# Splitting the first four loads of a gated attention-and-MLP kernel into two half transfers each, with a shorter TensorE filler

## The chip, the cores and the metric

The kernel runs on one core of one Trainium2 chip. The metric is device time in microseconds (us) of one execution of the whole program. Three runs of the kernel before took 259.8, 259.92 and 260.26 us, a median of 259.92 us.

## The reference, cut to what matters

The input x has 2048 tokens of 640 features in bf16. A gate g is the sigmoid of the row sum of x times gate_w. The output is g times a plus (1 - g) times b.

- a is linear attention with 32 heads of 20 features. qkv is x @ wqkv (640 by 1920), phi(t) is t + 1 for t > 0 and exp(t) otherwise, plus 1e-6. pk-transposed times v gives a 20 by 20 matrix per head, pq times that is divided by pq times the column sum of pk, and the result goes through wo.
- b is a two-part mixer: layernorm, w1, gelu, a shift of the four feature quarters by 1, -1, 2, -2 tokens, w2, residual; then layernorm, w3 (640 to 1728), gelu, w4, residual.

The part that this case touches is the beginning of a: q = x @ wq, where wq is the first 640 columns of wqkv.

```
qkv = (x @ wqkv).reshape(B, S, 3, H, Dh)
pq, pk = phi(q), phi(k)
```

## The kernel before, in words

**Tiling.** Tokens are cut into 16 tiles of 128 rows, features into 5 slices of 128. TensorE contracts over 128 partitions, so q for one token tile is the sum of five steps, one for each feature slice k: the transposed x tile `xT[:, k, tile]` as weights, the weight slice `wq[:, k, :]` as the moving operand, 512 columns and then 128 columns into two PSUM banks. So a step needs the x tile, transposed, and rows 128k to 128k+127 of wq.

**Loads.** Lines 694 to 715 issue the loads in a fixed order, each with a semaphore of its own, on the queue of SyncE (SP) or that of ScalarE (ACT). SP has, in order, x0, x1, wq2, x2, wk0, x3, wk2, wk4, x4, then a DMA transpose of x tile 3 (`x_turn`, line 690), which waits for x3, then the rest of x. ACT has wq0, wq1, wq3, wq4, wk1, wk3, and its first activation comes after them. Each of these loads is 128 rows of 1280 bytes, 160 KB. GpSimd (POOL) loads gate_w and fills small constants. ScalarE and SyncE issue their transfers by instructions of their own, in program order.

**TensorE's order in the first stage.** It is written out by hand (lines 945 to 950). `warmup` (line 871) issues filler matmuls on constants, which need no load: `WARM` = 3456 columns (line 770) as six matmuls of 512 columns and three of 128. Then `t_x(0)` (line 773) transposes x tile 0 by TensorE, first one block of 128 columns into one bank and then four into another, and VectorE copies each out to `xT` (line 779). After a second filler of 128 columns (`WARM2`) comes `q_three` (line 930), whose order is

```
order = [(0, 0), (1, None), (0, 1), (1, 0), (1, 1), (0, 2), (1, 2), (0, 3), (2, None), (1, 3), (0, 4), (1, 4),
         (2, 0), (2, 1), (2, 2), (2, 3), (2, 4)]
```

where (t, k) is the step of token tile t with slice k, and (t, None) is the transposing of tile t. `stream` (line 907) issues these; lines 923 and 924 are the 512-column and the 128-column matmul of a step. Then `k_two` does the same for k with the wk slices (`wkg` in the profile) and `k_tile(2)` follows; from tile 3 on, q and k alternate and the DMA transposes supply `xT`.

**The planner.** The order of everything else is chosen while the program is built: `_Items.run` (line 336) takes, again and again, the item that a cost model says can start first on TensorE. That model (`simulate`, line 232) charges an issue of 500 ns and 330 bytes per ns to each load, and 0.834 ns a column to the first filler; so the loads and the filler are inputs to it. The PSUM bank of an item is chosen by the same model. Semaphore waits follow from a tracker of which rows and bytes each instruction reads and writes (`_collect`, line 122); at the end of the program GpSimd waits once on each load's semaphore (line 309).

Of the kernel before, what the change touches and what calls it, by code (L numbers as in the profile page):

```python
# [11 lines left out]
D = 640  # L12
# [404 lines left out]
def _build(nc, A_x, A_wqkv, A_wo, B_w1, B_w2, B_w3, B_w4, gate_w, out, dbg=None, stop=None):  # L417
    sch = _Sched(nc)
# [59 lines left out]
    x_tok = pa.alloc("x_tok", [128, NT, D], BF16)  # L478
# [20 lines left out]
    wq = ra.alloc("wq", [128, KD, D], BF16)  # L499
# [77 lines left out]
    def dve(fn, reads, writes, cost=None):  # L577
        if cost is None:
            n = nfree(writes[0])
            cost = 65.0 + n / 0.96  # L580
        return sch.op("dve", fn, reads, writes, cost=cost)
# [93 lines left out]
    x2 = A_x[0]  # L675

    def dma_in(out_ap, in_ap, key, **kw):
        return sch.dma("sp", out_ap, in_ap, key, **kw)

    def load_x(t):  # L680
        dma_in(x_tok[:, t, :], x2[128 * t:128 * (t + 1), :], "x%d" % t)

    def load_wq(k, queue):
        sch.dma(queue, wq[:, k, :], A_wqkv[128 * k:128 * (k + 1), 0:D], "wq%d" % k)
# [6 lines left out]

    gwr = xn[:, 1, 0:128]
    dve(lambda e: e.memset(gwr, 0.0), [], [gwr])
    load_x(0)
    load_wq(0, "act")
    load_x(1)
    load_wq(1, "act")
    load_wq(2, "sp")
    load_wq(3, "act")
    load_x(2)  # L700
# [66 lines left out]
        assert tags.get((buf, sl)) == what, ("stale ring slot", buf, sl, what, tags.get((buf, sl)))  # L767

    IT = _Items()
    WARM = 3456  # L770
    WARM2 = 128

    def t_x(t):
        for k0, k1 in ((0, 1), (1, KD)) if t < 2 else ((0, KD),):
            b = bank()
            tr_group(b, [x_tok[:, t, 128 * k:128 * (k + 1)] for k in range(k0, k1)])
            if t == 2:
                mm_group(ps[:, b, 448:448 + KD], [(gwr, ident[:, 0:KD])])
            copy(dve, xT[:, k0:k1, 128 * t:128 * (t + 1)], psb(b, 0, 128 * (k1 - k0)).rearrange("p (k c) -> p k c", k=k1 - k0))
            if t == 2:  # L780
                copy(dve, wkg[:, :, D + 1:D + 2], ps[:, b, 448:448 + KD].rearrange("p (k o) -> p k o", o=1))
# [89 lines left out]
    def warmup(cols, cyc):  # L871
        b = bank()
        one = nc.const_aps.tensor(1.0, [128, 512], BF16)
        steps = [512] * (cols // 512) + [128] * (cols % 512 // 128)

        def fn(e):
            ins = None
            for n in steps:
                ins = e.matmul(ps[:, b, 0:n], one[:, 0:128], one[:, 0:n], start=True, stop=True)
            return ins  # L880
        pe(fn, [], [ps[:, b, :]], cost=cols * cyc)
# [60 lines left out]
    def addA(name, dur, fn, deps=()):  # L942
        IT.add("A", name, dur, fn, deps)

    addA(("warm",), 0.0, lambda: warmup(WARM, 0.834))
    addA(("tx", 0), 0.28, lambda: t_x(0))
# [478 lines left out]
def bass_gated_mix__linear_attn_block__mixer_s_mlp__prompt_kernel(  # L1425
    nc, A_x, A_wqkv, A_wo, B_x, B_w1, B_w2, B_w3, B_w4, gate_w, out
):
    assert tuple(A_x.shape) == (1, S, D) and tuple(out.shape) == (1, S, D)
    assert tuple(A_wqkv.shape) == (D, 3 * D) and tuple(A_wo.shape) == (D, D)
    assert tuple(B_w1.shape) == (D, D) and tuple(B_w2.shape) == (D, D)  # L1430
    assert tuple(B_w3.shape) == (D, F) and tuple(B_w4.shape) == (F, D) and tuple(gate_w.shape) == (D,)
    _build(nc, A_x, A_wqkv, A_wo, B_w1, B_w2, B_w3, B_w4, gate_w, out)
# [28 lines left out]
```

## Time and profile before

| what | value |
|---|---|
| three runs | 259.8, 259.92, 260.26 us |
| median | 259.92 us |
| profiled execution, first to last instruction (the only time recorded of it) | 258.2 us |
| median less that span | 1.7 us |
| TensorE busy | 253.3 us, 98% of the span |
| VectorE, ScalarE, GpSimd busy | 144.1, 108.2, 90.2 us |
| bytes read from HBM, written | 12.04 MB, 2.62 MB |

In the profile's rows a time is counted from the first instruction of the span, "PE" is a TensorE matmul, "PEld" its weight load, "SPq" and "ACTq" are the queues on which SyncE and ScalarE issue transfers. A matmul's duration is modelled with its pipeline's tail, so the rate of TensorE is read from the spacing of its rows and not from their durations. The bracket at the end of a row tells how long the engine sat idle before it and what ended that.

### The profile page before, as it was taken

To read this page: it belongs to the slowest core of one execution; us is meant where nothing else is said; L and a number is where in the kernel's file an instruction comes from. 1 tells how busy PE (TensorE), PEld (TensorE's weight loads), DVE (VectorE), ACT (ScalarE), POOL (GpSimd) and SP (SyncE) were. 2 spreads that over 40 slices of the span, in tenths; PEclk is the share of its full clock that TensorE was granted. 3 is DMA by queue.
4 is the path that set the end of the run, shared out by engine and by line. 5 is a ranking of instruction groups with operands and counts; after the bars stand their busy time and mean duration, and the time that the engine had idled before them with its cause. 6 is when DMAs were issued, how large, how long until landed. Compare 5 with 4: busy or idle time off the path is not lost.

```text
span 258.2 us, 3930 instructions
## 1 busy us (share of the span) xinstructions
PE 253.3 (98%) x1485; PEld 126.3 (49%) x1512; DVE 144.1 (56%) x284; ACT 108.2 (42%) x221; POOL 90.2 (35%) x144
## 2 busy tenths in 40 slices
PE   8999999999999999999999999999999999999996
PEld 3555555544454554555444445444444744445554
DVE  2588888899963993679999600399600033200023
ACT  1396676751366868675854331001540100253000
POOL 5012399967952152658917000133100021300000
PEclk9999999999999999999999999999999999999999
DMA  7766699646636699454636630114200022200011
GB/s 220 209 152 208 119 162 201 185 93 127 126 77 79 120 393 301 85 85 71 127 49 108 122 63 3 30 25 127 53 0 0 3 55 77 102 3 0 0 53 52
DMA packets 55891, 26.25 MB, mean 102 GB/s; under 512 B 47252, under 2 KB 54461, under 8 KB 55872
## 3 DMA queue, kind: packets, MB, share of 16 engines
q1 hardware_dynamic: 53696, 21.61, 37.4%
q0 software_dynamic: 1168, 3.28, 5.9%
q10 hardware_dynamic: 1008, 1.11, 1.2%
q8 instruction: 12, 0.20, 0.3%
q14 instruction: 7, 0.06, 0.1%
HBM read 12.04 MB, written 2.62 MB: 57 GB/s over the span
## 4 chain that ended last, share of the span: by engine, by line
PE 95%; DMA 2%; ACT 1%; issue 1%; DVE 0%; SPq 0%
PE ps L604 51%; PE ps L1216 30%; PE ps L806 8%; DMA wq<-in_A_wqkv_dram 2%; PE ps L923 2%; PE ps L1251 1%; ACT hsT L660 1%; PE ps L1129 1%; PE ps L924 1%; DVE x_tok L643 0%; PE ps L1010 0%; PE ps L1039 0%; ACT junk L659 0%; SPq L285 0%; PE ps L615 0%
## 5 line engine op out<-in xcount | busy, mean ns | idle before, releaser
L604 PE MATMUL ps<-xnT,w 128*128 128x512 bf16 x350 | 80.0, 379 | 0.5 <-issue 0.2
L643 DVE SCALAR_TENSOR_TENSOR x_tok<-ps,stg,abx 128x512 bf16<-128x512 f32 (+1 forms) x20 | 13.3, 670 | 80.6 <-PE ps L1216 58.6
L660 ACT ACTIVATE h2T<-ps 128x512 bf16<-128x512 f32 x52 | 30.5, 598 | 61.6 <-PE ps L604 61.5
L604 PEld LDWEIGHTS ps<-xnT,w 128*128 128x128 bf16 x360 | 34.6, 98 | 39.7 <-issue 0.5
L1216 PE MATMUL ps<-w,h2T 128*128 128x512 bf16 (+1 forms) x254 | 47.7, 346 | 0.3
L626 POOL TENSOR_SCALAR xn<-x_tok,st 128x640 bf16<-128x640 bf16 x32 | 35.1, 1105 | 26.0 <-DMA xnT<-xn 25.3
L626 POOL TENSOR_SCALAR abx<-x_tok,stg 128x640 f32<-128x640 bf16 x16 | 15.0, 945 | 70.8 <-DVE x_tok L643 70.8
L1216 PEld LDWEIGHTS ps<-w,h2T 128*128 128x128 bf16 x260 | 23.2, 98 | 24.5 <-issue 0.3
L660 ACT ACTIVATE Er<-ps 128x640 bf16<-128x640 f32 (+1 forms) x35 | 22.9, 662 | 15.4 <-PE ps L604 10.0
L659 ACT ACTIVATE junk<-x_tok 128x640 bf16<-128x640 bf16 x32 | 23.6, 739 | 2.8 <-DVE x_tok L641 2.5
L660 ACT ACTIVATE hsT<-ps 128x512 bf16<-128x512 f32 (+1 forms) x32 | 19.0, 594 | 11.2 <-PE ps L604 10.8
L604 PE MATMUL ps<-w,hsT 128*128 128x128 bf16 (+1 forms) x159 | 23.5, 298 | 0.2
L604 PE MATMUL ps<-wkg,xT 128*128 128x512 bf16 (+1 forms) x138 | 21.3, 298 | 0.1
L641 DVE SCALAR_TENSOR_TENSOR x_tok<-ps,x_tok 128x640 bf16<-128x640 f32 x16 | 13.1, 821 | 12.2 <-ACT junk L659 7.7
L1216 PE MATMUL ps<-M_sb,pqnT 128*128 128x512 bf16 (+1 forms) x98 | 19.6, 347 | 0.1
L604 PEld LDWEIGHTS ps<-w,hsT 128*128 128x128 bf16 x160 | 13.3, 98 | 12.3
L1158 DVE TENSOR_TENSOR pq_tok<-pq_tok,dnr 128x300 bf16<-128x300 bf16 (+1 forms) x48 | 17.7, 421 | 0.6
L806 PE MATMUL ps<-pk_tok,x_tok 128*128 128x512 bf16 x78 | 17.6, 379 | 0.1
L604 PEld LDWEIGHTS ps<-wkg,xT 128*128 128x128 bf16 x140 | 11.9, 97 | 11.2
L634 DVE TENSOR_TENSOR qprod<-qprod,pk_tok 128x640 f32<-128x640 f32 x13 | 16.3, 1252 | 0.5
L604 PE MATMUL ps<-wq,xT 128*128 128x512 bf16 (+1 forms) x69 | 16.2, 367 | 0.1
L626 DVE TENSOR_SCALAR Er<-Er 128x640 bf16<-128x640 bf16 (+1 forms) x35 | 12.1, 346 | 6.9 <-ACT Er L660 6.3
(89 smaller groups left out, 235.7 us busy)
## 6 DMA issues: line engine op xcount, KB each, us to landing
w<-in_B_w_dram SPq DMA_DIRECT2D x1, 2160.0 KB, 9.8
w<-in_B_w_dram SPq DMA_DIRECT2D x1, 2080.0 KB, 15.4
out_dram<-x_tok SPq DMA_DIRECT2D x3, 640.0 KB, 3.2
x_tok<-in_A_x_dram SPq DMA_DIRECT2D x1, 1280.0 KB, 6.5
w<-in_B_w_dram POOLq DMA_DIRECT2D x8, 160.0 KB, 4.5
x_tok<-in_A_x_dram SPq DMA_DIRECT2D x5, 160.0 KB, 5.2
wv<-in_A_wqkv_dram POOLq DMA_DIRECT2D x1, 800.0 KB, 5.6
wq<-in_A_wqkv_dram ACTq DMA_DIRECT2D x4, 160.0 KB, 4.3
```

The source lines that it names most:

```text
L604: ins = e.matmul(out_ap, l, r, start=(i == 0), stop=(i == n - 1))
L626: return engf(lambda e: e.tensor_scalar(out_ap, in_ap, s1, s2, op0, op1), rd, [out_ap], cost=cost)
L634: return engf(lambda e: e.tensor_tensor(out_ap, a, b_, op), [a, b_], [out_ap], cost=cost)
L641: return dve(lambda e: e.scalar_tensor_tensor(out_ap, in0, scalar, in1, op0, op1, accum_out=accum), rd, [out_ap, accum], cost=cost + 70.0)
L643: return dve(lambda e: e.scalar_tensor_tensor(out_ap, in0, scalar, in1, op0, op1), rd, [out_ap], cost=cost)
L659: return act(lambda e: e.activation(out_ap, in_ap, func, bias=bias, scale=scale, accum_out=accum), rd, wr, cost=cost)
L660: return act(lambda e: e.activation(out_ap, in_ap, func, bias=bias, scale=scale), rd, wr, cost=cost)
L806: ins = e.matmul(o, l, r, start=(t0 + q_ == 0), stop=(t0 + q_ == NT - 1))
L923: e.matmul(ps[:, b, 0:512], l, w[:, k, 0:512], start=(k == 0), stop=(k == KD - 1))
L924: return e.matmul(ps[:, b + 1, 0:n2], l, w[:, k, 512:512 + n2], start=(k == 0), stop=(k == KD - 1))
L1158: dve(lambda e, o=o, i0=i0, i1=i1: e.tensor_tensor(o, i0, i1, ALU.mult), [i0, dnr[:, 1, sd, :]], [o], cost=cost)
L1216: ins = e.matmul(o, l, r, start=first and i == 0, stop=last and i == len(prs) - 1, skip_group_check=True)
```

## The change

The four loads x0, wq0, x1, wq1 become eight. Each is cut into rows 0 to 63 and rows 64 to 127; the first half goes on SyncE's queue and the second on ScalarE's, each with its own semaphore. The order on both queues is x0, wq0, x1, wq1; all later loads keep their queue and order behind them. The first filler is 2944 columns, that is five matmuls of 512 and three of 128. Nothing else in the source differs.

```diff
-    load_x(0)
-    load_wq(0, "act")
-    load_x(1)
-    load_wq(1, "act")
+    for t in range(2):
+        for dst, src, key in ((x_tok[:, t, :], x2[128 * t:128 * (t + 1), :], "x%d" % t),
+                              (wq[:, t, :], A_wqkv[128 * t:128 * (t + 1), 0:D], "wq%d" % t)):
+            for h, queue in enumerate(("sp", "act")):
+                rows = slice(64 * h, 64 * (h + 1))
+                sch.dma(queue, dst[rows], src[rows], "%s%s" % (key, "ab"[h]))
     load_wq(2, "sp")
     load_wq(3, "act")
     load_x(2)
@@
-    WARM = 3456
+    WARM = 2944
```

## The prediction

> **What bounds the kernel now.** I read the page's shares first, then the chain of work that ended last, then the first 9 us engine by engine, and last the DMA issues with their time to landing. From the page:
>
> ```profile
> PE 253.3 (98%) x1485; PEld 126.3 (49%) x1512; DVE 144.1 (56%) x284; ACT 108.2 (42%) x221; POOL 90.2 (35%) x144
> PE 95%; DMA 2%; ACT 1%; issue 1%; DVE 0%; SPq 0%
> ```
>
> TensorE is the bound, so the change can pay only where TensorE waits. The chain, asked for the first 8 us, says where that is:
>
> ```profile
> 0.79 0.40 SPq L285
> 1.26 0.41 SPq L285
> 1.71 4.82 DMA wq<-in_A_wqkv_dram
> 6.57 0.39 PE ps L923
> ...
> 7.56 0.36 PE ps L615 x5
> ```
>
> The reader is to see that the end hangs neither on x0, x1, wq0 or wq1 nor on the filler. It hangs on the load that SP issues third, wq2, out at 1.71 and in at about 6.52; from 6.57 on the chain is TensorE. TensorE's own rows, and ScalarE's:
>
> ```profile
> 0.83 3.04 PE L879 MATMUL ps<-const-bfloat16-1.0 128*128 128x512 bf16 x9 [0.83 <-PEq L1446]
> ...
> 5.71 0.39 PE L923 MATMUL ps<-wq,xT 128*128 128x512 bf16 x1
> 5.93 0.22 PE L924 MATMUL ps<-wq,xT 128*128 128x128 bf16 x1
> 6.57 0.39 PE L923 MATMUL ps<-wq,xT 128*128 128x512 bf16 x1 [0.42 <-DMA wq<-in_A_wqkv_dram]
> ...
> 7.47 0.45 PE L615 MATMUL ps<-ident,x_tok 128*128 128x128 bf16 x5
> ```
> ```profile
> 1.21 0.15 PEld L879 LDWEIGHTS ps<-const-bfloat16-1.0 128*128 128x128 bf16 x1 [0.27 <-issue]
> 1.64 0.15 PEld L879 LDWEIGHTS ps<-const-bfloat16-1.0 128*128 128x128 bf16 x1 [0.28 <-issue]
> ...
> 3.81 0.28 PEld L615 LDWEIGHTS ps<-ident,x_tok 128*128 128x128 bf16 x5 [0.22 <-DMA x_tok<-in_A_x_dram]
> ```
> ```profile
> 3.65 1.28 ACT L660 ACT_TABLE_LOAD   x1 [3.65 <-issue]
> 8.53 1.30 ACT L660 ACTIVATE Er<-ps 128x640 bf16<-128x640 f32 x2 [3.59 <-PE ps L924]
> ```
>
> To be seen: the filler's rows stand 0.43 us apart for 512 columns; the last filler row starts at 3.56; tile 0 is transposed from 3.81, when x0 is in; step (1,1) starts at 5.71; step (0,2) waits for wq2 until 6.57; tile 2 is transposed at 7.47, just after x2 lands. Last the loads and the load on the DMA engines:
>
> ```profile
> x_tok<-in_A_x_dram SPq DMA_DIRECT2D x1, 160.0 KB, 3.0
> wq<-in_A_wqkv_dram ACTq DMA_DIRECT2D x1, 160.0 KB, 3.2
> wq<-in_A_wqkv_dram SPq DMA_DIRECT2D x1, 160.0 KB, 4.8
> ...
> x_tok<-in_A_x_dram SPq DMA_DIRECT2D x1, 160.0 KB, 5.2
> ```
> ```profile
> 3.00:4.00 1.00, 1.00 (x9) 0.50 (x7) 0.00 (x0) 0.35 (x1) 0.84 (x4) 1.00 1.06 386
> 7.00:8.00 1.00, 1.00 (x12) 0.57 (x10) 0.01 (x1) 0.00 (x0) 0.00 (x0) 1.00 1.06 383
> ```
>
> The last two columns of the second fence are the busy share of the 16 DMA engines and GB/s. From 3 to 8 us the engines are full at 310 to 386 GB/s: loads are served out of a backlog, and what lands when is decided by the bytes ahead of it.
>
> **The change part by part.** By the trace's landing records x0 is whole at 3.77, wq0 3.95, x1 4.51, wq1 4.78, wq2 6.52, wq3 6.73, x2 7.42, wq4 7.63.
>
> 1. The halves. x0 and wq0 are issued 0.01 apart and are served packet by packet in turn, one 1280-byte packet taking 55 ns on one of 16 engines, 8 packets of each load on every engine. With both halves of x0 ahead of wq0, an engine is done with x0 after 8 packets instead of 15: 7 x 55 ns = 0.39 us, so x0 is whole at 3.38. wq0 has the same 16 packets ahead and stays at 3.95. x1 becomes 4.12 by the same 0.39, wq1 stays. The least the halves can bring is nothing (the two halves end together no earlier than the whole), the most is 0.44, half the 0.88 us in which a pair of loads is served at 372 GB/s.
>
> 2. Four more issues, two on each queue. SP's rows are 0.47 apart, ACT's too, so wq2, x2, wk0, x3, wk2, wk4, x4 and, on ACT, wq3, wq4, wk1, wk3 are issued 0.94 later: wq2 at 2.65. The cover is the backlog. A first packet follows its issue by 1.03 us on SP (0.79 to 1.82), which makes wq2 ready at 3.68; the four tiles before it keep the engines until 4.51 (wq1's landing less the 0.27 that a landing takes). It is 0.83 early, so the price is 0. With that cover gone it would be the whole delay less 0.83. What the split adds to the backlog is four completion packets per engine at 9 ns: 0.04 us on wq2 and all behind it. Behind them on SP the transpose of tile 3 waits for x3 until 8.96 and SP's last early issue moves from 4.71 to 5.65, so nothing shifts; POOL issues only gate_w, unmoved. ScalarE's table load moves from 3.65 to 4.59 and ends at 5.87, before its first activation at 8.53: nothing. GpSimd's four more waits at the program's end and TensorE's second wait on a half (a wait row takes 0.05) lie beside the waits on loads: nothing.
>
> 3. The filler. 512 columns less is one row of 0.43 us. The last row starts at 3.13 instead of 3.56 and ends about 3.24, 0.14 before x0. If x0 comes no earlier, TensorE idles there and loses nothing, since it waits again for wq2.
>
> 4. TensorE up to wq2. Tile 0 is transposed at 3.42 instead of 3.82; (0,0) then waits for wq0, 4.0 instead of 4.46; (0,1) waits for wq1, 4.82 instead of 5.03; (1,1) starts after the copies of tile 1, between 0.2 and 0.4 earlier, at about 5.4. All of this arrives at the same wait: (0,2) needs wq2, which lands at 6.52 + 0.04. The early 0.3 turns into a wait on wq2 of 0.7 to 0.8 instead of 0.42. Then (1,2), (0,3), and x2 at 7.46 as before.
>
> Sum against the profiled execution: 258.2 + 0.04 = 258.24, the 0.4 off the filler and the 0.39 off x0 being given back at wq2. The median is 1.7 above that span, carried over: 259.92 + 0.04 = 259.96.
>
> [...] Here the rows above come first: x0 and wq0 on two queues share the engines and land 0.18 apart. [...] On the filler the rows show half rate up to 3.56 and 0.056 us for 128 columns from 3.82. [...]
>
> **The rivals.**
>
> A, faster: wq2's straggler does not come back. Fifteen of wq2's sixteen parts were in by 5.50 and one at 6.52, and x2 had twelve parts in by 6.39 and the last at 7.42. For it: at 372 GB/s nothing else holds wq2 beyond 5.5, and the runs differ by 0.46. Against: wq2 and all behind it keep queue and order, so whatever slowed that engine is met again. Then TensorE goes through: (1,1) ends 5.7, (0,2), (1,2), (0,3) take 0.81, x2 at 6.43, tile 2 is transposed at 6.55 instead of 7.47: 0.92 off, 259.0. If only half of the lag goes, 259.5. If the runs before had no straggler either, both kernels lose it and the start's 0.3 is kept: 259.6.
>
> B, slower: a descriptor slot per transfer. ACT's first packet comes at 2.26 for an issue at 0.80, SP's at 1.82 for one at 0.79. If one maker serves both queues in 0.43 us per transfer whatever its rows, wq2 is the ninth and not the fifth: ready at 1.82 + 8 x 0.43 = 5.26, past the 4.51 at which the engines want it. wq2 is 0.75 late, TensorE with it: 260.7. It decides once a transfer of 64 rows costs over 0.33 us there ((4.51 - 1.82) / 8). Against: at the end of the program an ACT store and an SP store issued 0.32 apart start their packets 0.37 apart.
>
> C, slower: TensorE's clock opens late. The full rate came 2.9 us after the filler began. If the shorter filler fails to open it and the count starts again with tile 0 at 3.4, it opens at 6.3; the half-rate work until then (2.9 us for 1.45 at full rate) ends with (1,0), and (1,1) is done by 6.6, still under the wait on wq2: price 0. If it opens another 2.9 later, at 9.2, half of the time from 6.57 on is lost: 1.3, 261.2. It decides from an opening at about 6.6. For it: the idle 0.14 and a filler of 2.45 us instead of 2.9. Against: the transposes fill the gap.
>
> D: the planner's order or banks change, since its filler is 0.43 us shorter. Either sign, about 0.5, by the spread of the runs; the items' order hangs on TensorE's own progress nearly everywhere, which speaks against it.
>
> **How the numbers follow.** Forecast 0.55 (own range 259.6 to 260.2, with the price of 0.04 and the case without stragglers), A 0.22, B 0.09, C 0.07, D 0.07. The time is the forecast's, 259.96. About 0.2% (0.52 us) is what a measurement of this kernel can tell from no change: faster is below 259.40, slower above 260.44. Faster: A with its end at 259.0, less the part that stops short, and half of D: 0.23. Slower: B, the dear end of C, half of D and a straggler that is worse: 0.19. The rest, 0.58, is the same. The range leaves out no more than 2 in 10: from A at 259.0 to B at 260.8.
>
> **What would show it.** Right: x0 whole near 3.4 and x1 near 4.1 with wq0, wq1 unmoved; tile 0 transposed near 3.4; a longer wait on wq2 ending near 6.57; tile 2 at 7.5. Wrong: wq2 landing well before 6.5 (A) or after 7 (B); rows 0.11 us apart for 128 columns after 4 (C); later rows in another order (D). It would also be wrong if x0 lands no earlier, though not the time.

## The result, and the profile after

The kernel after took a median of 262.2 us over nine runs (260.91 to 263.7). The kernel before, run beside it, took 259.8 us (259.04 to 261.43). The ratio is 1.0097 with a 95% interval of 1.0076 to 1.0117: about 2.5 us slower. The forecast was 259.96, its range ended at 260.8, and the chance given to slower was 0.19. The profiled execution has a span of 261.4 us and took 262.65; the span before was 258.2, so 3.2 us are to be found in it.

The page of the kernel after, span, shares and the chain by engine:

```profile
span 261.4 us, 3963 instructions
PE 256.4 (98%) x1511; PEld 127.2 (49%) x1511; DVE 144.5 (55%) x284; ACT 108.2 (41%) x221; POOL 90.6 (35%) x144
PE 96%; DMA 2%; SPq 1%; DVE 0%; issue 0%
```

The shares tell nothing yet. The order of the instructions on each engine, apart from the loads, the waits for them and the one filler matmul less, is that of before (for TensorE read from the weight loads, 1512 before and 1511 now, since some matmul records of before are missing), so the 3.2 us are no new plan. The chain of the first microseconds (start, duration, what) has changed:

```profile
0.79 0.60 SPq L285
...
1.45 0.82 SPq L285
...
2.31 0.61 SPq L285
...
2.97 0.61 SPq L285
...
3.63 4.70 DMA wq<-in_A_wqkv_dram
...
8.37 0.61 PE ps L925
```

Before, two issues of 0.40 stood ahead of wq2. Now there are four of 0.60 to 0.82: wq2 goes out at 3.63 instead of 1.71 and is whole at 8.33 instead of 6.52. TensorE's rows:

```profile
0.83 2.61 PE L881 MATMUL ps<-const-bfloat16-1.0 128*128 128x512 bf16 x8 [0.83 <-PEq L1448]
3.51 0.72 PE L615 MATMUL ps<-ident,x_tok 128*128 128x128 bf16 x5
...
4.33 0.51 PE L925 MATMUL ps<-wq,xT 128*128 128x512 bf16 x1
...
6.16 0.45 PE L615 MATMUL ps<-ident,x_tok 128*128 128x128 bf16 x5 [1.27 <-DMA x_tok<-in_A_x_dram]
6.74 0.39 PE L925 MATMUL ps<-wq,xT 128*128 128x512 bf16 x1
...
8.37 0.61 PE L925 MATMUL ps<-wq,xT 128*128 128x512 bf16 x1 [0.64 <-DMA wq<-in_A_wqkv_dram]
8.78 0.31 PE L926 MATMUL ps<-wq,xT 128*128 128x128 bf16 x1
...
9.95 0.74 PE L615 MATMUL ps<-ident,x_tok 128*128 128x128 bf16 x5
...
13.14 0.38 PE L925 MATMUL ps<-wkg,xT 128*128 128x512 bf16 x1
```

Tile 0 is transposed 0.3 early, as the change allows. Then TensorE waits 1.27 for x1, which before it did not, and 0.64 for wq2. The first step with wk, the last row shown, starts at 13.14; before it was at 9.96:

```profile
9.96 0.38 PE L923 MATMUL ps<-wkg,xT 128*128 128x512 bf16 x1
```

That difference, 3.18, is the whole loss of this execution; everything later is only shifted. It has two parts. The wait on wq2 ends 1.80 later (8.37 against 6.57). And from 8.37 a 512-column matmul has its successor 0.39 to 0.43 behind it instead of 0.22: the clock records give full speed from 4.60, half from 8.02 and full again from 11.43. The remaining 1.38 is this half-rate stretch, which at most can cost half of its 3.06 us, 1.5.

Loads and what the DMA engines did (DMA issues with KB each and median time to landing; then granted clock, DMA share and GB/s as the last columns of a table by stretch, four rows of after and one of before):

```profile
x_tok<-in_A_x_dram SPq DMA_DIRECT2D x2, 80.0 KB, 3.2
x_tok<-in_A_x_dram ACTq DMA_DIRECT2D x2, 80.0 KB, 2.7
wq<-in_A_wqkv_dram ACTq DMA_DIRECT2D x2, 80.0 KB, 3.2
wq<-in_A_wqkv_dram SPq DMA_DIRECT2D x2, 80.0 KB, 3.3
wq<-in_A_wqkv_dram SPq DMA_DIRECT2D x1, 160.0 KB, 4.7
```
```profile
3.00:4.00 1.00, 0.94 (x9) 0.67 (x8) 0.16 (x1) 0.00 (x0) 0.84 (x4) 1.00 0.86 232
4.00:5.00 1.00, 0.89 (x6) 0.20 (x3) 0.48 (x2) 0.00 (x0) 0.72 (x5) 1.00 0.82 205
5.00:6.00 1.00, 0.00 (x0) 0.00 (x0) 0.00 (x0) 0.58 (x1) 0.00 (x0) 1.00 0.87 234
9.00:10.00 1.00, 1.00 (x6) 0.45 (x5) 0.00 (x0) 0.00 (x0) 0.00 (x0) 0.50 1.05 374
```
```profile
5.00:6.00 1.00, 1.00 (x10) 0.37 (x7) 0.63 (x2) 0.00 (x0) 0.00 (x0) 1.00 1.04 310
```

A half takes about as long to land as a whole load did (3.0 before), and between 3 and 6 us the engines move 205 to 234 GB/s at a share of 0.82 to 0.87, where before they were full at 310 to 386. The share says less than it seems to. By the packet records the ordinary packet of 1280 bytes took 55 ns, as before. But of the 524 that started between 3 and 6 us 50 took over 100 ns, and these hold 0.28 of the engines' time; before it was 19 of 820, and 0.08. What holds them up is not shown. The first packet on SP's queue started at 2.43, before at 1.82. By the landing records the tiles were whole at

| load | before | after |
|---|---|---|
| x0, wq0 | 3.77, 3.95 | 3.46, 4.28 |
| x1, wq1 | 4.51, 4.78 | 6.11, 6.70 |
| wq2, wq3 | 6.52, 6.73 | 8.33, 6.90 |
| x2, wq4 | 7.42, 7.63 | 9.42, 8.53 |

Only x0 came earlier. Between 9 and 10 us, the last row of after in the table, the rate is back at 374, and the granted clock beside it reads 0.50.

### The profile page after: what moved, and what is told of

Same layout as the page of the kernel before. It is cut to its first block, busy times and chain, and to the rows that moved or that the text cites. A ratio compares the mean times of both kernels' runs of the same rounds, so it can differ in the third digit from the quotient of the medians.

```text
span 261.4 us, 3963 instructions
## 1 busy us (share of the span) xinstructions
PE 256.4 (98%) x1511; PEld 127.2 (49%) x1511; DVE 144.5 (55%) x284; ACT 108.2 (41%) x221; POOL 90.6 (35%) x144
## 4 chain that ended last, share of the span: by engine, by line
PE 96%; DMA 2%; SPq 1%; DVE 0%; issue 0%
PE ps L604 52%; PE ps L1218 30%; PE ps L808 8%; PE ps L925 2%; DMA wq<-in_A_wqkv_dram 2%; SPq L285 1%; PE ps L1253 1%; PE ps L1131 1%; PE ps L926 1%; DVE x_tok L643 0%; PE ps L1012 0%; PE ps L1041 0%; PE ps L615 0%
## 5 line engine op out<-in xcount | busy, mean ns | idle before, releaser
L604 PE MATMUL ps<-xnT,w 128*128 128x512 bf16 x360 | 81.3, 379 | 0.0
L1218 PE MATMUL ps<-w,h2T 128*128 128x512 bf16 (+1 forms) x260 | 48.3, 347 | 0.0
L604 PE MATMUL ps<-w,hsT 128*128 128x512 bf16 (+1 forms) x160 | 23.7, 299 | 0.0
L604 PE MATMUL ps<-wkg,xT 128*128 128x130 bf16 (+1 forms) x140 | 21.4, 299 | 0.0
```

Of the source, the lines that this page charges most:

```text
L604: ins = e.matmul(out_ap, l, r, start=(i == 0), stop=(i == n - 1))
L1218: ins = e.matmul(o, l, r, start=first and i == 0, stop=last and i == len(prs) - 1, skip_group_check=True)
```

## The experiments

**Theories.** The leading one (theory 1 in the expectations): the eight transfers are issued too slowly, each queue needing about 0.65 us for a half of 80 KB, so the two queues supply at most 160 KB in 0.65 us, some 250 GB/s; the backlog that the prediction took as cover never forms, and wq2 is late by its own issue. Against it: that the filler or the clock costs the time (theories 3 and 2); that a tile on both queues is served badly (theory 4); that a descriptor slot shared by both queues is paid per transfer (theory 5, rival B of the prediction); that halves are served badly wherever they stand. Edits are shown against the kernel after or before, as said; each median is compared with runs of the kernel before on the same chip (259.3 to 259.7).

### The filler and the clock

The change with the long filler:

```diff
-    WARM = 2944
+    WARM = 3456
```

> The eight half transfers with the filler of before (3456 columns). Theory 1 (a 64-row transfer costs each queue 0.60 to 0.82 us to issue where a 128-row one costs 0.43, so wq2 goes out at 3.6 and the loads come late): as slow as the changed kernel, 262.2 within 0.5, wq2 issued near 3.6. Theory 3 (the shorter filler is at fault, by the clock or the idle before tile 0): back to 259.8 to 260.2.

Measured: 262.12 us, ratio 1.0103 (1.0072 to 1.0134). The loss stays. The kernel before with only the filler shortened:

```diff
-    WARM = 3456
+    WARM = 2944
```

> The whole transfers of before with the filler of 2944 columns. Theory 1: 259.8 within 0.3, tile 0 transposed at 3.8 as before, about 0.5 of idle ahead of it, wq2 issued at 1.71. Theory 3: 261 to 262.5, TensorE's rows at half rate beyond 4 us.

Measured: 259.51 us, ratio 1.0007 (0.9989 to 1.0025). The filler's cut costs nothing. TensorE's rows in this kernel:

```profile
3.86 0.71 PE L615 MATMUL ps<-ident,x_tok 128*128 128x128 bf16 x5 [0.42 <-DMA x_tok<-in_A_x_dram]
...
5.05 0.59 PE L615 MATMUL ps<-ident,x_tok 128*128 128x128 bf16 x5
5.47 0.38 PE L923 MATMUL ps<-wq,xT 128*128 128x512 bf16 x1
...
9.73 0.38 PE L923 MATMUL ps<-wkg,xT 128*128 128x512 bf16 x1
```

It waits 0.42 for x0 and runs at half rate (a 512-column row 0.38 ahead of the next and not 0.22) up to about 5.35, and still reaches wk at 9.73, earlier than before, because wq2 was in at 5.78. In the change with the long filler the same rows read:

```profile
5.26 0.61 PE L925 MATMUL ps<-wq,xT 128*128 128x512 bf16 x1 [0.75 <-DMA wq<-in_A_wqkv_dram]
...
7.18 0.61 PE L925 MATMUL ps<-wq,xT 128*128 128x512 bf16 x1 [0.68 <-DMA wq<-in_A_wqkv_dram]
...
12.02 0.63 PE L925 MATMUL ps<-wq,xT 128*128 128x512 bf16 x1
12.45 0.31 PE L926 MATMUL ps<-wq,xT 128*128 128x128 bf16 x1
```

With more filler than the change and less waiting on loads (0.75 and 0.68 against 1.27 and 0.64), the rows stay 0.4 apart until 12.5, and wk begins at 14.03. So the half rate does not hang on the filler being short. Nor does waiting bring it by itself: further down, the kernel with four extra loads of 128 rows waits 1.22 for wq2 and goes on at full rate, and the one with halves behind a backlog waits for no load and is at half rate until about 6.4. What decides it is not shown. To take the half rate away, TensorE was kept busy with more filler while it waits, 16 matmuls of 128 columns before tile 1 and 12 before (0,2) (kernel after, `None, None` is a filler item):

```diff
-        order = [(0, 0), (1, None), (0, 1), (1, 0), (1, 1), (0, 2), (1, 2), (0, 3), (2, None), (1, 3), (0, 4), (1, 4),
+        order = [(0, 0)] + [(None, None)] * 8 + [(1, None), (0, 1), (1, 0), (1, 1)] + [(None, None)] * 6 + [(0, 2), (1, 2), (0, 3), (2, None), (1, 3), (0, 4), (1, 4),
```

> The changed kernel with 16 small filler matmuls after step (0, 0) and 12 ahead of step (0, 2), so that TensorE works while it waits for x1 and wq2. Theory 2 (the loss is the clock that closes from 8.0 to 11.4 us because TensorE idles): 1.3 to 1.5 us faster than the changed kernel, 260.8, granted clock 1.000. Theory 1: the loads still end the waits, so 262.2 less at most the share of runs in which the clock closed (3 of 9 runs, 1.4 us each): 261.7 to 262.2.

Measured: 261.70 us, ratio 1.0085 (1.0057 to 1.0114). In its profile every step is at full rate (0.22 to 0.23 from a 512-column row to the next) and wk begins at 11.93, 2.0 later than before: with the clock out of it, that is the part of the loads (some of it this filler's own doing, since x1 was in at 5.16 and transposed at 6.02). In the median no more than 0.5 comes off, and the interval overlaps that of the change. So the half rate is 1.4 us of the profiled execution. What it is of the median is not isolated, since the filler that took it away also took time of its own.

### The direction of the cut, and the queues

The change with column halves (128 rows of 640 bytes) in place of row halves:

```diff
-                rows = slice(64 * h, 64 * (h + 1))
-                sch.dma(queue, dst[rows], src[rows], "%s%s" % (key, "ab"[h]))
+                cols = slice(320 * h, 320 * (h + 1))
+                sch.dma(queue, dst[:, cols], src[:, cols], "%s%s" % (key, "ab"[h]))
```

> Each of the four loads in two halves by columns (128 rows of 640 bytes) and not by rows, same queues, order and short filler. Theory 1 (the row count makes the issue dear): issues of 0.43 us again, wq2 out at 2.65, x0 in by 3.4, 259.8 to 260.3. If two transfers in place of one are dear by themselves, or packets are served slowly whenever one tile is on both queues: 261.5 to 263.

Measured: 260.96 us, ratio 1.0062 (1.0032 to 1.0091). SyncE's issues in this kernel, and two stretches of its table:

```profile
0.79 0.40 SPq L285 DMA_DIRECT2D x_tok<-in_A_x_dram  x1
1.26 0.42 SPq L285 DMA_DIRECT2D wq<-in_A_wqkv_dram  x1
1.72 0.43 SPq L285 DMA_DIRECT2D x_tok<-in_A_x_dram  x1
2.19 0.91 SPq L285 DMA_DIRECT2D wq<-in_A_wqkv_dram  x2
```
```profile
3.00:4.00 1.00, 1.00 (x11) 0.80 (x10) 0.23 (x1) 0.00 (x0) 0.83 (x4) 1.00 1.03 244
4.00:5.00 1.00, 0.70 (x4) 0.13 (x2) 0.42 (x1) 0.38 (x1) 0.73 (x5) 1.00 0.91 187
```

With 128 rows the issue is back at 0.40 to 0.43 and wq2 goes out at 2.67, as the prediction had assumed for the change (2.65). About 1 us of the loss goes. But wq2 lands at 7.33, not at 6.56, and x2 at 9.07: 187 to 255 GB/s between 3 and 6 us. TensorE's last wait is the one on x2:

```profile
9.11 0.45 PE L615 MATMUL ps<-ident,x_tok 128*128 128x128 bf16 x5 [0.76 <-DMA x_tok<-in_A_x_dram]
```

So the dear issue is one part of the loss, and the cut at this place the other, even at the price that the prediction had. A little of the second part is the smaller packet: one of 640 bytes took 32 ns where one of 1280 took 55, which is an estimated 0.3 us for the four tiles (1024 packets of the one against 512 of the other, on 16 engines). Next, whether it matters that a tile lies on both queues: row halves with x on SP and wq on ACT, and the same with column halves. Both against the kernel after, the column variant with the row variant's head:

```diff
-        for dst, src, key in ((x_tok[:, t, :], x2[128 * t:128 * (t + 1), :], "x%d" % t),
-                              (wq[:, t, :], A_wqkv[128 * t:128 * (t + 1), 0:D], "wq%d" % t)):
-            for h, queue in enumerate(("sp", "act")):
+        for dst, src, key, queue in ((x_tok[:, t, :], x2[128 * t:128 * (t + 1), :], "x%d" % t, "sp"),
+                                     (wq[:, t, :], A_wqkv[128 * t:128 * (t + 1), 0:D], "wq%d" % t, "act")):
+            for h in range(2):
```
```diff
-                rows = slice(64 * h, 64 * (h + 1))
-                sch.dma(queue, dst[rows], src[rows], "%s%s" % (key, "ab"[h]))
+                cols = slice(320 * h, 320 * (h + 1))
+                sch.dma(queue, dst[:, cols], src[:, cols], "%s%s" % (key, "ab"[h]))
```

> Eight 64-row halves as in the change and the short filler, but both halves of a tile on one queue, x on SP, wq on ACT, as before the change. The column halves have shown that the row count makes the issue dear (0.43 us an issue again) and that 1.4 us of the loss stays nevertheless. Theory 1 (dear issues): wq2 still goes out near 3.6 and the time is that of the change, 261.7 to 262.5. Theory 4 (one tile on both queues is served slowly, 156 to 281 GB/s between 3 and 6 us where whole tiles get 320 to 390): 260.5 to 261, the rate held back by the issues alone, at most 252 GB/s.

> Eight column halves (128 rows of 640 bytes), both halves of a tile on one queue, short filler. Theory 4 (both queues in one tile): 259.5 to 259.9, 320 GB/s or more from 3 to 8 us. If smaller packets or more transfers are slow by themselves: 260.7 to 261.3 as with column halves on two queues.

Measured: rows 262.67 us, ratio 1.0126 (1.0101 to 1.0151), wq2 out at 3.60 and in at 8.46; columns 260.51 us, ratio 1.0044 (1.0021 to 1.0068), wq2 out at 2.65 and in at 6.95. Both are near their partners on two queues. Theory 4 falls.

### One operand, one tile, finer pieces

Only x0 and x1 cut by rows (first edit, against the kernel after), and only wq0 and wq1 (second):

```diff
-            for h, queue in enumerate(("sp", "act")):
-                rows = slice(64 * h, 64 * (h + 1))
-                sch.dma(queue, dst[rows], src[rows], "%s%s" % (key, "ab"[h]))
...
+        for h, queue in enumerate(("sp", "act")):
+            rows = slice(64 * h, 64 * (h + 1))
+            sch.dma(queue, x_tok[rows, t, :], x2[128 * t + 64 * h:128 * t + 64 * (h + 1), :], "x%d%s" % (t, "ab"[h]))
+        load_wq(t, ("act", "sp")[t])
```
```diff
+        sch.dma(("sp", "act")[t], x_tok[:, t, :], x2[128 * t:128 * (t + 1), :], "x%d" % t)
+        for h, queue in enumerate(("sp", "act")):
+            rows = slice(64 * h, 64 * (h + 1))
+            sch.dma(queue, wq[rows, t, :], A_wqkv[128 * t + 64 * h:128 * t + 64 * (h + 1), 0:D], "wq%d%s" % (t, "ab"[h]))
```

> Only x0 and x1 in two 64-row halves over both queues, wq0 whole on ACT and wq1 whole on SP behind them, short filler. Theory 1: two dear issues on SP (1.32 us) and one plain one, wq2 out at 2.6, half of the loss: 260.5 to 261.2. If it is the weights' halves that cost: 259.5 to 260.

> Only wq0 and wq1 in two 64-row halves over both queues, x0 whole on SP and x1 whole on ACT, short filler. Theory 1: wq2 out at 2.6 as with x alone, the same 260.5 to 261.2. If it is x's halves that cost: 259.5 to 260.

Measured: x 262.19 us, ratio 1.0111 (1.0062 to 1.0159), wq2 out 2.94 and in 8.07; wq 260.88 us, ratio 1.0064 (1.0041 to 1.0088), wq2 out 2.51 and in 7.21. The parts do not add up: four halves already cost what eight do (x) or two thirds of it (wq). In both kernels most of the whole loads issued among or just behind the halves took 0.59 to 0.65 as well, one 0.74. In the profile with x cut TensorE stayed at half rate (0.38 to 0.43 from a 512-column row to the next) until about 13. The smallest cut, x0 alone and by columns:

```diff
+    for h, queue in enumerate(("sp", "act")):
+        cols = slice(320 * h, 320 * (h + 1))
+        sch.dma(queue, x_tok[:, 0, cols], x2[0:128, cols], "x0%s" % "ab"[h])
+    load_wq(0, "act")
+    load_x(1)
+    load_wq(1, "act")
```

> Only x0 cut, into two column halves, one on each queue; wq0, x1, wq1 whole as before; short filler. Theory 5: one transfer more on ACT and one start more, 0.33: 259.6 to 260.0, x0 in by 3.4, wq2 0.2 to 0.4 later. Theory 1 alone: 259.3 to 259.6.

Measured: 259.92 us, ratio 1.0016 (0.9991 to 1.0042); x0 in at 3.32, 0.45 earlier than before, wq2 out at 1.72 and in at 5.53. An early x0 alone is worth nothing here. Each of the four tiles in four transfers of 32 rows (kernel after):

```diff
-            for h, queue in enumerate(("sp", "act")):
-                rows = slice(64 * h, 64 * (h + 1))
-                sch.dma(queue, dst[rows], src[rows], "%s%s" % (key, "ab"[h]))
+            for h in range(4):
+                rows = slice(32 * h, 32 * (h + 1))
+                sch.dma(("sp", "act")[h % 2], dst[rows], src[rows], "%s%s" % (key, "abcd"[h]))
```

> The change with each of the four tiles in four transfers of 32 rows, two on each queue: the suspected cost doubled, the bytes the same. Theory 1: 16 issues of 0.6 us, wq2 out at about 6.1 instead of 3.6, the engines at 130 GB/s or less until then, 2 to 3 us slower than the change: 264 to 265.5. If a transfer of fewer rows is dear only once or the loss is in the service: 262 to 263.

Measured: 262.1 us, ratio 1.0094 (1.0072 to 1.0116): less than the 264 to 265.5 that theory 1 expected. SyncE's issues:

```profile
0.79 0.87 SPq L285 DMA_DIRECT2D x_tok<-in_A_x_dram  x2
1.70 0.89 SPq L285 DMA_DIRECT2D wq<-in_A_wqkv_dram  x2
```

Two issues in 0.87: 32 rows take 0.41 to 0.44, not 0.6 or more. The price does not grow as the rows get fewer; 64 rows are the dear ones among 128, 64 and 32. wq2 goes out at 4.49 and lands at 8.05, and while two queues supply 80 KB in 0.47 us, 170 GB/s, the engines move 136 to 260 between 3 and 7 us. This fits the supply side of theory 1 at another size.

### The price of an issue alone

Sixteen loads of 32 bytes a row ahead of everything, eight of 128 rows and then eight of 64, in turn on both queues (kernel before; `zb` is scratch):

```diff
+    for i in range(16):
+        n = 128 if i < 8 else 64
+        sch.dma(("sp", "act")[i % 2], zb[0:n, 16 * i:16 * (i + 1)], x2[0:n, 16 * i:16 * (i + 1)], "tiny%d" % i)
```

> The kernel before with 16 extra loads of 32 bytes a row ahead of its first load, in turn on SP and ACT: eight of 128 rows, then eight of 64. A measurement of issue and start alone, with next to no bytes. Theory 1 alone (dear issues, each queue for itself): issues of 0.43 us with 128 rows and 0.60 with 64, landings as far apart as the issues, a pair every 0.47 and every 0.65 us. Theory 5 (both queues share something that takes about 0.33 us per transfer whatever its bytes, read from the halves' first landings): a pair every 0.65 us or slower in both series.

Measured: 265.4 us (one run); by construction everything is late, and only the spacings count. With 128 rows the issues are 0.47 apart; the first landings on SP come at 2.20, 2.64, 3.31 and 3.70 and on ACT 0.17 to 0.19 behind each (between the second and the third GpSimd's gate load starts). So, that stretch aside, a pair of transfers, one on each queue, starts every 0.39 to 0.45. With 64 rows issues take 0.55 to 0.65 (one 0.87) and pairs start every 0.62 to 0.69. No slot of 0.33 or more stands for each transfer whatever its rows: rival B's mechanism, theory 5, falls. With 64 rows the pairs come no faster than the issues, so a slot of that size for 64 rows alone is not excluded. The issue's price by rows stands without any bytes to speak of.

Four of these loads put between wq1 and wq2, with all tiles whole, first of 64 rows and then of 128 (kernel before):

```diff
+    for i in range(4):
+        sch.dma(("sp", "act")[i % 2], zb[0:64, 16 * i:16 * (i + 1)], x2[0:64, 16 * i:16 * (i + 1)], "tiny%d" % i)
```
```diff
+    for i in range(4):
+        sch.dma(("sp", "act")[i % 2], zb[0:128, 16 * i:16 * (i + 1)], x2[0:128, 16 * i:16 * (i + 1)], "tiny%d" % i)
```

> The kernel before with four extra loads of 64 rows and 32 bytes a row between wq1 and wq2, two on each queue: four more transfers as in the change, the first four whole. Theory 1 alone: wq2 goes out near 3.0 and is ready before the engines have served wq1, so 259.5 to 259.9. Theory 5: four more slots of 0.33 us push wq2 and all behind it about 0.5 to 1.0 back, 260 to 260.6. If what costs is that the first tiles are cut: 259.5.

> The same with 128 rows in the four extra loads, whose issue takes 0.43 us. Theory 1 alone: 259.3 to 259.7, nothing lost. Theory 5: as with 64 rows, 260 to 260.6.

Measured: 64 rows 260.83 us, ratio 1.0032 (1.0009 to 1.0055); 128 rows 260.14 us, ratio 1.0004 (0.9981 to 1.0027). SyncE's issues, with 64 rows and with 128:

```profile
1.71 1.47 SPq L285 DMA_DIRECT2D zb<-in_A_x_dram  x2
3.21 0.61 SPq L285 DMA_DIRECT2D wq<-in_A_wqkv_dram  x1
```
```profile
1.71 0.91 SPq L285 DMA_DIRECT2D zb<-in_A_x_dram  x2
2.65 0.43 SPq L285 DMA_DIRECT2D wq<-in_A_wqkv_dram  x1
```

In the median, four more issues of 0.47 behind whole tiles cost nothing that can be told from zero (the interval reaches to 0.7 us), as the prediction's step 2 had it for issues of that price. The profiled execution, the third slowest of ten (260.63), does not show the cover of that step, though: wq2 came in at 7.47, TensorE waited 1.22 for it, and wk began at 10.89, 0.93 later than before.

```profile
7.52 0.39 PE L925 MATMUL ps<-wq,xT 128*128 128x512 bf16 x1 [1.22 <-DMA wq<-in_A_wqkv_dram]
7.75 0.22 PE L926 MATMUL ps<-wq,xT 128*128 128x128 bf16 x1
```

Four of 64 rows cost 0.8. The load behind them is dear too: wq2, of 128 rows, takes 0.61 there.

### Eight halves behind a backlog

The first six loads (x0, x1, wq0 to wq3) whole, and x2, wq4, wk0 and wk1 in row halves (kernel before):

```diff
-    load_x(2)
-    load_wq(4, "act")
-    load_wk(0, "sp")
-    load_wk(1, "act")
+    for dst, src, key in ((x_tok[:, 2, :], x2[256:384, :], "x2"), (wq[:, 4, :], A_wqkv[512:640, 0:D], "wq4"),
+                          (wkg[:, 0, 0:D], A_wqkv[0:128, D:2 * D], "wk0"), (wkg[:, 1, 0:D], A_wqkv[128:256, D:2 * D], "wk1")):
+        for h, queue in enumerate(("sp", "act")):
+            rows = slice(64 * h, 64 * (h + 1))
+            sch.dma(queue, dst[rows], src[rows], "%s%s" % (key, "ab"[h]))
```

> The kernel before with x0, wq0, x1, wq1, wq2, wq3 whole and the next four loads, x2, wq4, wk0, wk1, cut into 64-row halves over both queues: the same four extra issues of 0.6 us and the same eight halves, but behind a backlog of about 2 us that the engines have still to serve. If the halves cost because the engines run dry at the start (theory 1 with the rate that the issues allow, 160 KB per 0.65 us = 252 GB/s): the rate stays above 300 GB/s from 3 to 8 us, 259.5 to 260.1. If halves are served slowly wherever they stand: 260.8 to 262.

Measured: 259.85 us, ratio 1.0012 (1.0001 to 1.0024). The time is that expected for halves behind a backlog, the rate is not:

```profile
3.00:4.00 1.00, 1.00 (x8) 0.58 (x7) 0.00 (x0) 0.00 (x0) 0.83 (x4) 1.00 1.08 382
6.00:7.00 1.00, 1.00 (x7) 0.49 (x6) 0.14 (x1) 0.94 (x1) 0.00 (x0) 1.00 1.09 279
```

Eight halves of the same size, as dear to issue (0.56 to 0.64 each, one 0.87), cost 0.3 us here instead of 2.5. The engines stay full while they are served, though at 279 GB/s, where the whole tiles of before moved at 350 in the same microsecond, so these halves moved more slowly than whole tiles though nothing waited for issue. TensorE waits for no load, and still its rows are 0.4 apart until about 6.4:

```profile
6.01 0.61 PE L924 MATMUL ps<-wq,xT 128*128 128x512 bf16 x1
6.43 0.24 PE L925 MATMUL ps<-wq,xT 128*128 128x128 bf16 x1
6.51 0.38 PE L924 MATMUL ps<-wq,xT 128*128 128x512 bf16 x1
6.73 0.22 PE L925 MATMUL ps<-wq,xT 128*128 128x128 bf16 x1
```

Two things differ from the cut at the start: a backlog stands in front, and TensorE needs these tiles later (x2 was in at 7.00, tile 2 was transposed at 7.60). The time alone does not part them. The rate speaks for the first, 279 to 315 GB/s between 5 and 8 us against 205 to 234 between 3 and 6 in the change. Column halves in the same place (against the kernel just shown):

```diff
-            rows = slice(64 * h, 64 * (h + 1))
-            sch.dma(queue, dst[rows], src[rows], "%s%s" % (key, "ab"[h]))
+            cols = slice(320 * h, 320 * (h + 1))
+            sch.dma(queue, dst[:, cols], src[:, cols], "%s%s" % (key, "ab"[h]))
```

> As late_split with column halves (128 rows of 640 bytes). If partitions decide: limited by the 640-byte packets alone, which took 32 ns in the other column kernels, so 300 to 330 GB/s with few slow packets. If it is the number of transfers: 275 to 300.

Measured: 259.45 us (one run), 314 to 345 GB/s between 5 and 8 us. To see whether the 64 neighbouring partitions are what slows the halves, even and odd rows were tried in their place, in the late cut and in the change:

```diff
-            rows = slice(64 * h, 64 * (h + 1))
+            rows = slice(h, 128, 2)
```

> As late_split, but the halves of x2, wq4, wk0, wk1 are the even and the odd rows, so that each half is spread over all partitions; a measurement of the rate from 5.5 to 8 us, where halves of consecutive rows got 276 to 299 GB/s with the engines busy. If halves are slow because each goes to half of the partitions: 350 GB/s or more. If 64-row transfers are slow by their number or size: 275 to 300 again.

> The change with halves of even and odd rows in place of rows 0 to 63 and 64 to 127. If partitions decide the service, what is left is the issue of 0.6 us and its 252 GB/s: wq2 out at 3.6, in about 7.5, 260.5 to 261.3. If not: as the change, 261.8 to 262.5.

Measured: 263.75 us for the late ones (one run) and 265.71 us, ratio 1.0241 (1.021 to 1.0272), for the change with even and odd rows. Neither tells anything on partitions. The program's own tracker takes alternate rows as overlapping, so each odd half waited for the landing of its even half (ACT's first half went out at 3.15 instead of 0.81). What they show is the price of putting halves in series. The late one again without that false wait, the waits reckoned from neighbouring rows and the transfer then exchanged for one of alternate rows (the same rows in all):

```diff
             rows = slice(64 * h, 64 * (h + 1))
             sch.dma(queue, dst[rows], src[rows], "%s%s" % (key, "ab"[h]))
+            waits, fn, sem = sch.prog[queue][-1]
+            sch.prog[queue][-1] = (waits, lambda e, o=dst[h:128:2], i=src[h:128:2]: e.dma_start(o, i), sem)
```

> As late_split with even and odd rows in the halves of x2, wq4, wk0, wk1, issued on both queues with no wait between them. Read is the rate from 5.5 to 8 us. If halves are slow behind a backlog because each goes to half of the partitions: 340 GB/s or more in place of 276 to 299, few packets over 85 ns. If it is 64 rows as such: 275 to 300. The time stays near 259.7 either way, since TensorE does not wait there.

Measured: 259.69 us (one run). By half microseconds from 5.5 to 8 it moved 377, 323, 277, 297, 312 GB/s against 277, 279, 279, 300, 279 with neighbouring rows. That is neither the 340 expected of the one nor the rate of the other. The packets tell more: of those of 1280 bytes that started in this stretch the median took 55 ns, as with whole tiles, against 72 with neighbouring rows, and 19 of 619 took over 85 ns against 74 of 552. So behind a backlog halves of neighbouring rows go with slower packets, by one execution of each kernel; the partitions and the rows in memory alternate together here, so which of them does it is not told apart. In the change the median packet took 55 ns, so this is not what slows its halves.

## Why the prediction was wrong

**What bounds the kernel.** Right: the end still hangs on wq2, issued on SP behind x0 and x1 (now also behind halves of wq0 and wq1).

**Step 1, the halves.** x0 was taken to come in at 3.38 and came at 3.46: right. wq0 was to stay at 3.95 and came at 4.28. x1 was to come at 4.12 and came at 6.11, and wq1 at 6.70 instead of 4.78. The working shared the engines out in packets and took the packets as there; from x1 on it failed with step 2.

**Step 2, the issues: the step that failed.** It went wrong at two numbers. It took an issue from rows of 128-row loads, 0.47 apart; issues of 64 rows are 0.59 to 0.86 apart, and wq2 went out 1.92 later and not 0.94. (The first packet on SP's queue followed its issue by 1.64 and not 1.03, too. And the 0.27 taken for a landing is not what the trace of before shows for wq1: its last completion packet ran at 4.35, 0.43 ahead of its landing at 4.78.) By the step's own formula for the cover gone, "the whole delay less 0.83", that alone is 1.92 - 0.83 = 1.1, or 261 us. Then the cover: 0.83 us of backlog assumed that the four tiles keep the engines busy at the rate of before, 372 GB/s, while they are themselves supplied by the slower issues. The kernel with column halves had the issue that the step assumed, wq2 out at 2.67, and still lost 1.6 us. Tried in parts: four more issues at 0.47 with whole tiles 0 (ratio 1.0004), at 64 rows 0.8 (1.0032), the cut at the start with plain issues 1.1 to 1.6 (1.0044, 1.0062), the cut with dear ones 2.5 to 3.3 (1.0097, 1.0126), eight dear halves behind a backlog 0.3 (1.0012). So the dear issue is shown: by rows against columns it is some 1 us on two queues and 2 us on one. The rest is open. That the engines lack work at the start fits the row halves (524 packets at 55 ns would fill 0.60 of the engines' time between 3 and 6 us), but it is argued and not shown, and it fits the column halves badly: between 3 and 4 us the engines are busy there at a share of 1.03 and move 244 GB/s, with a supply of up to 340 (160 KB in 0.47 us). In both, packets of over 100 ns hold 0.27 to 0.28 of the engines' time between 3 and 6 us, against 0.08 before.

**Step 3, the filler.** Right: the short filler alone gives a ratio of 1.0007.

**Step 4.** Tile 0 was transposed at 3.51 (3.42 predicted). The wait on x1, 1.27, was not foreseen; the wait on wq2 ended at 8.37 and not 6.57, tile 2 came at 9.95 and not 7.5.

**The rivals.** B was right in place, a start that is too slow for the engines, and in its sign, wq2 after 7; it was too small in size (260.7) and wrong in its mechanism. C priced a late clock at 1.3 us and hung it on the short filler. The half rate cost 1.38 in the profile, but that the two are close is luck: the clock had opened at 4.60 and fell back at 8.02, and with the long filler it opened only after 12.5. A's price was too high: wq2 came in at 5.78 with the short filler and at 5.82 with alternate rows behind a backlog, and wk began 0.23 and 0.52 earlier than before, not 0.92 (the first of the two at half rate up to 5.35). D did not happen.

**The halves as a whole.** x0 did come in 0.31 earlier, at 3.46 instead of 3.77, and the kernel still lost 2.5 us (ratio 1.0097): cutting the four loads at the start of the program brought a loss, not merely no gain.

None of the variants beat the kernel before beyond what the measurement can tell: 1.0007 with the short filler, 1.0016 with x0 in column halves, one run of 259.45 with late column halves.

## What to carry to other kernels

Take the duration of an issue from a row of the very shape (here 0.47 apart with 128 rows, 0.59 to 0.86 with 64), and work a backlog out from the supply after the change (bytes of an issue over the distance to the next, summed over the queues), as an upper bound, and not from the rate before it. Do not cut the first loads of a program without a trial: eight halves cost 2.5 us there, and 0.3 behind six whole loads, where they were also needed later. A load that lands late can cost more than its lateness: in the profile wq2 ended its wait 1.80 later, and 3.18 were lost, the other 1.38 at half rate behind it.

## What the runs showed of the hardware

- Issue by rows: among the first loads on SP and on ACT one of 128 rows took 0.39 to 0.48 us, of 64 rows 0.53 to 0.65 (single ones 0.48 to 0.49 and 0.82 to 0.87), of 32 rows 0.41 to 0.44. Most loads of 128 rows just behind or among those of 64 rows took 0.59 to 0.65. From its eighth load on, SP's queue had single issues of 128 rows at 0.50 to 0.71 in kernels without any of 64 rows (0.59 before, 0.71 with column halves). Why 64 rows are the dear ones is open.
- Of two loads issued at the same moment on both queues, with little to move, ACT's began to land 0.17 to 0.19 after SP's with 128 rows and 0.27 to 0.37 with 64. Where GpSimd's gate load came between two pairs, they were 0.67 apart and not 0.39 to 0.45.
- The granted clock moved in stages of 3.41 us in the kernel after (full 4.60 to 8.02, half to 11.43). The mean granted clock of a run does not show a late opening: the run with the long filler reads 1.000, and its tables 1.00 in each microsecond from 2 to 13, with rows at half rate (0.38 to 0.43 from a 512-column row to the next) until 12.5. So the three runs of the kernel after with a mean of 0.993 cannot be taken as the only ones that lost time at half rate.
